# Routing scratch moved from SBUF into a PSUM bank, and the first batch's transforms set on other steps

## The chip, the cores and the metric

The kernel runs on one core of one Trainium2 chip. The metric is the device time of one execution in microseconds (us). An execution is also profiled: every instruction of the five engines has a start and an end. PE is TensorE's matrix multiply, PEld its weight load, DVE the vector engine, ACT the scalar engine, POOL the GpSimd engine, and SP the queue that only issues transfers.

## The reference

```python
X = np.fft.fft(np.fft.fft(x, axis=1), axis=2).real      # x: 8 x 3072 x 256
h = X.reshape(-1, 256) @ w_in                            # 256 -> 2048
y = (h * sigmoid(1.702 * h)) @ w_out                     # 2048 -> 256
do = y @ w_skip > 0                                      # only these rows go to an expert
e = argmax(y[do] @ w_gate, axis=1)                       # one of 8 experts
gate = softmax(y[do] @ w_gate)[e]
out = y;  out[do] += gate * (relu(y[do] @ w1[e]) @ w2[e])
```

## The kernel before

The work has two phases. **Phase 1** computes the Fourier transform, the first two-layer network and the routing; it fills the span up to about 1900 us. **Phase 2** runs the experts over the rows that phase 1 has scattered to memory.

Phase 1 goes over 8 batches, each cut in two half batches (the variable `hb`, 0 to 15). A half batch has three blocks of 512 tokens, and a block is worked off in 8 steps, so that a half batch has 24 steps and the whole has 384 (`main`, variable `g`). Products are split in high and low parts, so each is made of three matmuls.

A step consists of these pieces, in the order in which each engine's queue receives them:

- `hstep(g)`: 12 matmuls into the PSUM tiles `pt` (L855), then on DVE two instructions for `pp` (L859) and two for `h` (L861, L862).
- `ystep(g-2)`: 24 matmuls into the four accumulators `py` (L886), which use the step's `gh` and `gl`.
- `gelu(g)`: two activations on ACT (L869, L870), and on POOL the subtraction `gl` (L871, 128x1024 elements).
- After the last step of a block `finish` copies the four accumulators to `rows` (L894, DVE) while POOL sets one column of `rows` to zero (L891).
- The side list: whatever the dictionary `side` holds for this step, in the order in which it was appended. `plan` appends for all half batches before the loop starts; `finish` appends the routing of its block while the loop is written out. Nothing reorders these lists, and each engine runs its instructions strictly in this order.

The **routing** of a block stands in the side lists of the steps after its last one, in the order a1, a2, a3, four scatters, one step each:

- a1 is `route1`: six DVE instructions (L784 to L789) that find the best expert of each row and write the flags `oh` (128x32). Their scratch tiles `rm` and `rq` lie in SBUF. Then the transfer of `rows` to the output is issued on SP.
- a2 is `route2`: five small matmuls (L798, L800) with a triangle of ones, which count the rows in front of each row. They write a PSUM tile of the tag `misc`.
- a3 is `route3`: five DVE instructions (L810 to L814), which turn the counts into target rows.

The blocks are numbered from 0; the routing of block b has a1 in step 8b+10 of the whole count. A 49th, small routing handles 8 leftover tokens (`plan_mini`).

The tag `misc` has one PSUM bank and one buffer. Its other users are the **transforms** of the next half batch, `piece_mm` (L262): four per half batch, each with 9 matmuls (`p0` in `plan`), emptied one step later on DVE and ACT (`e0`, `e1`). A tile that takes the bank waits until every instruction that uses the tile before it is done.

POOL also folds the next batch's input (L212 to L224, L238 to L250), issues the scatters (L818) and the loads of the transform matrices (L202).

Of the kernel before, what the change touches and what calls it, by code (L numbers as in the profile page):

```python
# [12 lines left out]
F32 = mybir.dt.float32  # L13
# [5 lines left out]
ALU = mybir.AluOpType  # L19
AX = mybir.AxisListType  # L20
# [3 lines left out]
P = 128  # L24
# [140 lines left out]
class Phase1:  # L165
# [486 lines left out]
    def plan(self, hb):  # L652
        nc = self.nc
        b, odd = hb // 2, hb % 2
# [6 lines left out]
        st = {}  # L661
        if not odd:
# [8 lines left out]
            def p0(p):  # L671
                sh, sl = self.s
                q = self.piece_mm(st["cm"][4 + p % 2], sh, sl, p, KC)
                st["q"] = q
            def e0(p):
                st["xp"] = self.evac_odd0(b, p, st["q"])
            def e1(p):
                self.evac_odd1(p, st["xp"], st["q"], *st["y"], le)
            for p, s in enumerate((10, 13, 15, 21) if hb == 0 else (1, 5, 7, 13)):
                add(s, lambda p=p: p0(p))  # L680
                add(s + 1, (lambda p=p: e0(p)) if p % 2 == 0 else (lambda p=p: e1(p)))
            if b + 1 < self.nb:
# [65 lines left out]
        else:  # L748
# [14 lines left out]
                        self.cmn = self.cmn2  # L763
            def e0(p):
                self.evac_even(b + 1, p, st["q"], *st["y"], le)
            for p, s in enumerate((16, 18, 20, 22) if b == 0 else (8, 13, 15, 17)):
                add(s, lambda p=p: p0(p))
                add(s + 1, lambda p=p: e0(p))
            def sp(c):
# [4 lines left out]
                add(22 + c // 2 if b == 0 else 20 + c, lambda c=c: sp(c))  # L774


    def route1(self, rows, nt):
        nc, bp = self.nc, self.rp
        v = nc.vector
        sk, lg = rows[:, :nt, D], rows[:, :nt, D + 1 : D + 9]  # L780
        m = bp.tile([P, 4], F32, tag="rm", name="rm")
        q = bp.tile([P, 4, 8], F32, tag="rq", name="rq")
        oh = bp.tile([P, 4, 8], BF16, tag="roh", bufs=2, name="roh")
        v.tensor_reduce(m[:, :nt], lg, AX.X, ALU.max)  # L784
        v.tensor_tensor(q[:, :nt], lg, m[:, :nt].unsqueeze(2).to_broadcast([P, nt, 8]), ALU.is_ge)
        v.scalar_tensor_tensor(q[:, :nt], q[:, :nt], 16.0, self.k8[:, :nt], ALU.mult, ALU.add)
        v.tensor_reduce(m[:, :nt], q[:, :nt], AX.X, ALU.max)
        v.scalar_tensor_tensor(m[:, :nt], sk, 0.0, m[:, :nt], ALU.is_gt, ALU.mult)
        v.tensor_tensor(oh[:, :nt], q[:, :nt], m[:, :nt].unsqueeze(2).to_broadcast([P, nt, 8]), ALU.is_equal)  # L789
        return oh  # L790

    def route2(self, oh, nt):
        nc = self.nc
        ps = self.ps.tile([P, 512], F32, tag="misc", name="pmisc")
        o = oh[:, :nt].rearrange("p t e -> p (t e)")
        n = nt * 8
        mm = nc.tensor.matmul
        mm(ps[:, 0:n], lhsT=self.tri[:, 0], rhs=o, start=True, stop=False, skip_group_check=True)  # L798
        for i in range(nt):
            mm(ps[:, 8 * (i + 1) : n + 8], lhsT=self.tri[:, 1], rhs=o[:, : n - 8 * i], start=False, stop=i == nt - 1, skip_group_check=True)  # L800
        return ps

    def route3(self, rows, oh, ps, nt):
        nc, bp = self.nc, self.rp
        v = nc.vector
        q = bp.tile([P, 4, 8], F32, tag="rq", name="rq")
        m = bp.tile([P, 4], F32, tag="rm", name="rm")
        ix = bp.tile([P, 4], I32, tag="rix", bufs=2, name="rix")
        pv = ps[:, : nt * 8].rearrange("p (t e) -> p t e", t=nt)
        v.tensor_tensor(q[:, :nt], pv, self.base.unsqueeze(1).to_broadcast([P, nt, 8]), ALU.add)  # L810
        v.tensor_add(self.base, self.base, ps[:, nt * 8 : nt * 8 + 8])
        v.tensor_tensor(q[:, :nt], q[:, :nt], oh[:, :nt], ALU.mult)
        v.tensor_reduce(m[:, :nt], q[:, :nt], AX.X, ALU.add)
        v.tensor_scalar_add(ix[:, :nt], m[:, :nt], BIG)  # L814
        return ix
# [16 lines left out]
    def main(self):  # L832
        nc, tc, nb = self.nc, self.tc, self.nb
        v = nc.vector
        ps = self.ps
# [6 lines left out]
        bp = self.bp  # L842
        if True:
# [44 lines left out]
            def finish(gb, gnow):  # L888
                st = {}
                rows = self.rp.tile([P, 4, RW], F32, tag="rows", bufs=2, name="rows")  # L890
                nc.gpsimd.memset(rows[:, :, NW : NW + 1], 0.0)  # L891
                nc.gpsimd.tensor_scalar_add(rows[:, :, RW - 1 :], self.rid[:, 0, :, 1:], float(gb * TB))
                for t in range(4):
                    v.tensor_copy(rows[:, t, :NW], ys[gb][t])  # L894
                del ys[gb]

                def a1():
                    st["oh"] = self.route1(rows, 4)
                    nc.sync.dma_start(self.a["out"][gb * TB : (gb + 1) * TB].rearrange("(t p) d -> p t d", p=P), rows[:, :, :D])

                def a2():
                    st["ps"] = self.route2(st["oh"], 4)

                def a3():
                    st["ix"] = self.route3(rows, st["oh"], st["ps"], 4)

                left = nhb * NBLK - 1 - gb
                if left == 0:
                    self.last_block(a1, a2, a3, lambda t: self.scatter(rows, st["ix"], t))
                    return  # L910
                for i, f in enumerate((a1, a2, a3)):
                    self.side[gnow + 1 + i].append(f)
                for t in range(4):
                    self.side[gnow + 4 + (t // 2 if left == 1 else t)].append(lambda t=t: self.scatter(rows, st["ix"], t))
                if left == 1:
                    self.side[gnow + 5].append(pad0)
                if left == 2:
                    self.side[gnow + 8].append(self.ahead_load)
# [40 lines left out]
    def plan_mini(self, g0):  # L959
        nc, nb = self.nc, self.nb  # L960
        v = nc.vector
        st = {}

        def load():
            st["r"] = self.rp.tile([P, nb], F32, name="rmini")
            nc.sync.dma_start(st["r"], self.ydm.rearrange("b o -> o b").to_broadcast([P, nb]))
            st["m"] = [self.rp.tile([P, nb], F32R, name=f"m{i}") for i in range(2)]
            v.tensor_copy(st["m"][0], self.mini[:, :nb])
            v.tensor_sub(st["m"][1], self.mini[:, :nb], st["m"][0])

        def first():
            mh, ml = st["m"]
            ph = st["ph"] = self.ps.tile([P, NF, nb], F32, tag="misc", name="ph")
            for f in range(NF):
                for n, (w_, x_) in enumerate(((self.wch, mh), (self.wch, ml), (self.wcl, mh))):
                    nc.tensor.matmul(ph[:, f], lhsT=w_[:, 0, f * P : (f + 1) * P], rhs=x_, start=n == 0, stop=n == 2)

        def gelu():
            hm = self.rp.tile([P, NF, nb], F32, name="hm")
            v.tensor_mul(hm, self.w128.unsqueeze(2).to_broadcast([P, NF, nb]), st["r"].unsqueeze(1).to_broadcast([P, NF, nb]))  # L980
            v.tensor_add(hm, hm, st["ph"])
            nc.scalar.activation(hm, hm, AF.Gelu_apprx_sigmoid)
            st["g"] = [self.rp.tile([P, NF, nb], F32R, name=f"gm{i}") for i in range(2)]
            nc.scalar.copy(st["g"][0], hm)
            nc.gpsimd.tensor_sub(st["g"][1], hm, st["g"][0])

        def second():
            gh, gl = st["g"]
            py = st["py"] = self.ps.tile([P, NW], F32, tag="misc", name="pmini")
            for f in range(NF):  # L990
                for n, (x_, w_) in enumerate(((gh, self.woh), (gh, self.wol), (gl, self.woh))):
                    nc.tensor.matmul(py[:nb], lhsT=x_[:, f], rhs=w_[:, f], start=f == 0 and n == 0, stop=f == NF - 1 and n == 2)

        def rows():
            r = st["rows"] = self.rp.tile([P, 1, RW], F32, name="rowsm")
            v.memset(r[:, 0], 0.0)
            v.tensor_copy(r[:nb, 0, :NW], st["py"][:nb])

        def a1():
            r = st["rows"]  # L1000
            st["oh"] = self.route1(r, 1)
            v.tensor_scalar_add(r[:, 0, RW - 1 : RW], self.rid[:, 0, 0, 1:2], float(nb * S))
            nc.sync.dma_start(self.a["out"][nb * S : nb * S + nb], r[:nb, 0, :D])

        def a2():
            st["ps"] = self.route2(st["oh"], 1)

        def a3():
            st["ix"] = self.route3(st["rows"], st["oh"], st["ps"], 1)

        def sc():
            self.scatter(st["rows"], st["ix"], 0)

        for w, f in ((0, load), (4, first), (5, gelu), (7, second), (8, rows), (12, a1), (13, a2), (14, a3), (15, sc)):
            self.side[g0 + w].append(f)


# [388 lines left out]
```

## Time and profile before

| | |
|---|---|
| median of 3 runs | 2425.53 us (2424.12 to 2425.88) |
| profiled execution | 2424.24 us |
| its span in the trace | 2422.5 us |
| mean granted TensorE clock | 0.989 of full speed |

[...] Most executions agree within 0.1%, as the three times show.

### The profile page before, as it was taken

What the parts mean: (1) busy time and instruction counts of PE and PEld (TensorE: products, weight loads), DVE (VectorE), ACT (ScalarE), POOL (GpSimd) and SP (SyncE); (2) the same over time, 40 slices, a digit from 0 to 9 for tenths busy, and PEclk for the clock granted to TensorE, in tenths of its full rate; (3) what the DMA queues carried; (4) which work ended last, traced back from release to release, by engine and by line L of the source; (5) the groups of instructions that cost most, each with busy time, mean ns of one, the idle gap of its engine ahead of it and who ended that gap; (6) DMA issues with size and microseconds to landing.
All of it is one profiled execution on the core that took longest, in us unless ns stands there. A gap on an engine that the chain in (4) does not pass through costs nothing. (4 is left out here: it accounts for less than half of the span.)

```text
span 2422.5 us, 50479 instructions
## 1 busy us (share of the span) xinstructions
PE 2349.9 (97%) x19222; PEld 2320.0 (96%) x19222; DVE 1532.4 (63%) x3195; ACT 1095.8 (45%) x1355; POOL 1579.1 (65%) x1246
## 2 busy tenths in 40 slices
PE   5999999999999999999999999899999999999999
PEld 4899999999999999999999999899999999999999
DVE  7679676756665766576576757655657445555544
ACT  5544444444445454444544454445444333333332
POOL 3567688888878896878788888777666312323211
PEclk9999999999999999999999999999999999999999
DMA  7302311231122113112212121121101312323111
GB/s 259 116 34 77 122 55 37 68 124 37 65 91 77 39 60 130 37 37 86 104 53 69 59 100 47 55 89 39 62 20 33 107 44 84 115 84 113 40 43 41
DMA packets 91450, 178.83 MB, mean 74 GB/s; under 512 B 10895, under 2 KB 66750, under 8 KB 85104
## 3 DMA queue, kind: packets, MB, share of 16 engines
q1 hardware_dynamic: 69488, 96.12, 12.6%
q0 software_dynamic: 20448, 77.87, 9.4%
q8 instruction: 133, 2.18, 0.4%
q10 hardware_dynamic: 1312, 2.10, 0.3%
q14 instruction: 69, 0.57, 0.1%
HBM read 126.21 MB, written 66.59 MB: 80 GB/s over the span
## 5 line engine op out<-in xcount | busy, mean ns | idle before, releaser
L871 POOL TENSOR_TENSOR gl<-h,gh 128x1024 fp32r<-128x1024 f32 x384 | 923.8, 2406 | 352.2 <-ACT h L870 313.3
L869 ACT ACTIVATE gh<-h 128x1024 fp32r<-128x1024 f32 x384 | 407.4, 1061 | 890.0 <-DVE h L862 791.3
L886 PE MATMUL py<-woh,gh 128*128 128x264 f32 x3072 | 778.3, 287 | 0.7 <-DVE rows L894 0.7
L886 PE MATMUL py<-wol,gh 128*128 128x264 f32 x3072 | 775.6, 286 | 0.0
L859 DVE SCALAR_TENSOR_TENSOR pp<-rb,w,pt 128x256 f32<-128x256 f32 x768 | 334.0, 476 | 404.7 <-PE pt L855 404.2
L886 PEld LDWEIGHTS py<-woh,gh 128*128 128x128 f32 x3072 | 587.9, 191 | 1.1 <-issue 0.8
L886 PEld LDWEIGHTS py<-wol,gh 128*128 128x128 f32 x3072 | 586.6, 191 | 0.0
L886 PE MATMUL py<-woh,gl 128*128 128x264 f32 x3072 | 460.5, 284 | 1.0 <-POOL gl L871 1.0
L855 PE MATMUL pt<-yh,wch 128*128 128x256 f32 x1536 | 433.9, 283 | 3.3 <-DVE pp L859 2.6
L855 PE MATMUL pt<-yh,wcl 128*128 128x256 f32 x1536 | 429.3, 279 | 1.9 <-DVE wcl L431 1.9
L855 PE MATMUL pt<-yl,wch 128*128 128x256 f32 x1536 | 429.6, 280 | 0.7 <-POOL yl L296 0.5
L870 ACT ACTIVATE h<-h 128x1024 f32<-128x1024 f32 x384 | 407.7, 1062 | 35.2 <-ACT gh L869 0.7
L886 PEld LDWEIGHTS py<-woh,gl 128*128 128x128 f32 x3072 | 409.8, 189 | 1.2 <-POOL gl L871 1.2
L1287 POOL DMA_INDIRECT out<-ob,ix x82 | 79.9, 974 | 337.8 <-DVE ob L1301 335.7
L861 DVE TENSOR_TENSOR h<-pp,pt 128x512 f32<-128x512 f32 x384 | 264.2, 688 | 54.7 <-POOL gl L871 2.1
L855 PEld LDWEIGHTS pt<-yh,wch 128*128 128x128 f32 x1536 | 290.4, 189 | 4.4 <-DVE pp L859 3.0
L855 PEld LDWEIGHTS pt<-yh,wcl 128*128 128x128 f32 x1536 | 291.0, 189 | 2.1 <-DVE wcl L431 2.1
L855 PEld LDWEIGHTS pt<-yl,wch 128*128 128x128 f32 x1536 | 291.8, 190 | 1.1 <-POOL yl L296 0.7
L862 DVE TENSOR_TENSOR h<-pp,pt 128x512 f32<-128x512 f32 x384 | 261.2, 680 | 0.0
L818 POOL DMA_INDIRECT xs<-rows,rix x192 | 194.3, 1012 | 44.2 <-issue 26.9
L1309 PE MATMUL po<-w2h,hh 128*128 128x256 f32 x656 | 188.8, 288 | 0.0
L1273 PE MATMUL h<-xl,w1h 128*128 128x256 f32 x656 | 185.1, 282 | 2.3 <-issue 2.2
(230 smaller groups left out, 3487.5 us busy)
## 6 DMA issues: line engine op xcount, KB each, us to landing
cmat<-cm POOLq DMA_DIRECT2D x48, 1158.0 KB, 6.3
raw<-raw SPq DMA_DIRECT2D x48, 512.0 KB, 5.5
out<-rows SPq DMA_DIRECT2D x48, 512.0 KB, 3.2
r<-w SPq DMA_DIRECT2D x14, 1024.0 KB, 6.6
nx<-xs SPq DMA_DIRECT2D x33, 266.0 KB, 3.0
rb<-yd SPq DMA_DIRECT2D x48, 128.0 KB, 3.5
wide<-w_in SPq DMA_DIRECT2D x8, 512.0 KB, 8.7
wide<-w_out SPq DMA_DIRECT2D x8, 512.0 KB, 6.1
```

The source lines that it names most:

```text
L818: i = self.nc.gpsimd.indirect_dma_start(self.xs, bass.IndirectOffsetOnAxis(ap=ix[:, t : t + 1], axis=0), rows[:, t], None, bounds_check=E ...
L855: nc.tensor.matmul(pt[z][:, i], lhsT=w_[:, z, f], rhs=x_[:, z, cols], start=n == 0, stop=n == 2)
L859: v.scalar_tensor_tensor(pp[:, i], r, self.w128[:, 2 * s + i : 2 * s + i + 1], pt[0][:, i], ALU.mult, ALU.add)
L861: v.tensor_add(h[:, :, 0], pp, pt[1])
L862: v.tensor_sub(h[:, :, 1], pp, pt[1])
L869: nc.scalar.activation(gh, hv, AF.Gelu_apprx_sigmoid)
L870: nc.scalar.activation(hv, hv, AF.Gelu_apprx_sigmoid)
L871: nc.gpsimd.tensor_sub(gl, hv, gh)
L886: nc.tensor.matmul(ys[gb][t], lhsT=x_[:, i, tk], rhs=w_[:, 2 * s + i], start=s == 0 and part is hi and n == 0, stop=ends and part is lo an ...
L1273: nc.tensor.matmul(h[:, z], lhsT=w_[:, k, f * P : (f + 1) * P], rhs=x_[:, k], start=i == 0, stop=i == 5)
L1287: d = self.nc.gpsimd.indirect_dma_start(self.out, bass.IndirectOffsetOnAxis(ap=ix, axis=0), ob, None, bounds_check=self.ntok - 1, oob_is_e ...
L1309: self.nc.tensor.matmul(po[t], lhsT=x_[:, f, t * P : (t + 1) * P], rhs=w_[:, f], start=f == 0 and n == 0, stop=f == 7 and n == 2)
```

## The change

1. The scratch values `m` (4 columns) and `q` (32 columns) of the routing are columns 64 to 67 and 96 to 127 of the same PSUM tile into which the triangle matmuls write columns 0 to 39. So `route1` takes the `misc` bank in a1, a step earlier than before, and it is held until the end of a3.
2. One intermediate of `route1` stays in SBUF, as `k`. Before, it was written over `q`.
3. In the first half batch (hb 0) three of the transforms are set on steps 13, 15, 16 instead of 10, 13, 15 (the fourth stays at 21), and in the second (hb 1) on 16, 17, 21, 22 instead of 16, 18, 20, 22. The instructions that empty them follow one step later, as before, and so do the loads of the matrices that each `p0` of hb 1 issues.
4. The small routing of the leftover tokens moves by one step (12 to 15 becomes 13 to 16).

```diff
-            for p, s in enumerate((10, 13, 15, 21) if hb == 0 else (1, 5, 7, 13)):
+            for p, s in enumerate((13, 15, 16, 21) if hb == 0 else (1, 5, 7, 13)):
...
-            for p, s in enumerate((16, 18, 20, 22) if b == 0 else (8, 13, 15, 17)):
+            for p, s in enumerate((16, 17, 21, 22) if b == 0 else (8, 13, 15, 17)):
...
+    def scratch(self, ps):
+        return ps[:, 64:68], ps[:, 96:128].rearrange("p (t e) -> p t e", t=4)
+
     def route1(self, rows, nt):
...
-        m = bp.tile([P, 4], F32, tag="rm", name="rm")
-        q = bp.tile([P, 4, 8], F32, tag="rq", name="rq")
+        ps = self.ps.tile([P, 512], F32, tag="misc", name="pmisc")
+        m, q = self.scratch(ps)
         oh = bp.tile([P, 4, 8], BF16, tag="roh", bufs=2, name="roh")
         v.tensor_reduce(m[:, :nt], lg, AX.X, ALU.max)
         v.tensor_tensor(q[:, :nt], lg, m[:, :nt].unsqueeze(2).to_broadcast([P, nt, 8]), ALU.is_ge)
-        v.scalar_tensor_tensor(q[:, :nt], q[:, :nt], 16.0, self.k8[:, :nt], ALU.mult, ALU.add)
-        v.tensor_reduce(m[:, :nt], q[:, :nt], AX.X, ALU.max)
+        k = bp.tile([P, 4, 8], F32, tag="rq", name="rq")
+        v.scalar_tensor_tensor(k[:, :nt], q[:, :nt], 16.0, self.k8[:, :nt], ALU.mult, ALU.add)
+        v.tensor_reduce(m[:, :nt], k[:, :nt], AX.X, ALU.max)
         v.scalar_tensor_tensor(m[:, :nt], sk, 0.0, m[:, :nt], ALU.is_gt, ALU.mult)
-        v.tensor_tensor(oh[:, :nt], q[:, :nt], m[:, :nt].unsqueeze(2).to_broadcast([P, nt, 8]), ALU.is_equal)
-        return oh
+        v.tensor_tensor(oh[:, :nt], k[:, :nt], m[:, :nt].unsqueeze(2).to_broadcast([P, nt, 8]), ALU.is_equal)
+        return oh, ps
...
-    def route2(self, oh, nt):
+    def route2(self, oh, ps, nt):
         nc = self.nc
-        ps = self.ps.tile([P, 512], F32, tag="misc", name="pmisc")
...
     def route3(self, rows, oh, ps, nt):
...
-        q = bp.tile([P, 4, 8], F32, tag="rq", name="rq")
-        m = bp.tile([P, 4], F32, tag="rm", name="rm")
+        m, q = self.scratch(ps)
...
-        for w, f in ((0, load), (4, first), (5, gelu), (7, second), (8, rows), (12, a1), (13, a2), (14, a3), (15, sc)):
+        for w, f in ((0, load), (4, first), (5, gelu), (7, second), (8, rows), (13, a1), (14, a2), (15, a3), (16, sc)):
```

## Rows read from the trace of the kernel before

**Rows 1.** The page: busy time of each engine, share of the span, instructions.
```profile
PE 2349.9 (97%) x19222; PEld 2320.0 (96%) x19222; DVE 1532.4 (63%) x3195; ACT 1095.8 (45%) x1355; POOL 1579.1 (65%) x1246
```

**Rows 2.** Waits of PE: us in total, times, the longest.
```profile
PE pmisc L798 <- DVE roh L789: 25.1, 13, 4.3
...
PE pmisc L798 <- DVE yl L281: 2.1, 1, 2.1
...
PE pmisc L798 <- DVE xp L286: 0.5, 1, 0.5
```

**Rows 3.** DVE's routing lines: out<-in, count | busy us, mean ns | idle before.
```profile
L812 DVE TENSOR_TENSOR rq<-rq,roh 128x32 f32<-128x32 f32 (+1 forms) x49 | 58.6, 1196 | 0.0
L786 DVE SCALAR_TENSOR_TENSOR rq<-rq,k 128x32 f32<-128x32 f32 (+1 forms) x49 | 33.3, 680 | 1.7
L788 DVE SCALAR_TENSOR_TENSOR rm<-rows,rm 128x4 f32<-128x4 f32 x48 | 32.6, 678 | 1.7
L785 DVE TENSOR_TENSOR rq<-rows,rm 128x32 f32<-128x32 f32 x48 | 22.6, 471 | 1.7
L789 DVE TENSOR_TENSOR roh<-rq,rm 128x32 bf16<-128x32 f32 (+1 forms) x49 | 22.5, 458 | 1.7
L814 DVE TENSOR_SCALAR rix<-rm 128x4 int32<-128x4 f32 (+1 forms) x49 | 20.8, 424 | 1.7
...
L787 DVE TENSOR_REDUCE rm<-rq 128x4 f32<-128x32 f32 (+1 forms) x49 | 9.1, 186 | 1.7
L810 DVE TENSOR_TENSOR rq<-pmisc,base 128x32 f32<-128x32 f32 (+1 forms) x49 | 9.0, 183 | 0.0
```

**Rows 4.** DVE's timeline in blocks 19 and 38: start us, us, instruction [idle before <-releaser].
```profile
840.36 0.19 DVE L784 TENSOR_REDUCE rm<-rows 128x4 f32<-128x32 f32 x1 [3.59 <-POOL rows L891]
...
841.33 3.35 DVE L786 SCALAR_TENSOR_TENSOR rq<-rq,k 128x32 f32<-128x32 f32 x1
...
850.96 0.18 DVE L810 TENSOR_TENSOR rq<-pmisc,base 128x32 f32<-128x32 f32 x1
851.18 0.16 DVE L811 TENSOR_TENSOR base<-base,pmisc 128x8 f32<-128x8 f32 x1
851.26 1.09 DVE L812 TENSOR_TENSOR rq<-rq,roh 128x32 f32<-128x32 f32 x1
...
1555.52 5.17 DVE L785 TENSOR_TENSOR rq<-rows,rm 128x32 f32<-128x32 f32 x1
```

**Rows 5.** POOL's timeline beside block 19's routing, same columns.
```profile
841.88 2.33 POOL L871 TENSOR_TENSOR gl<-h,gh 128x1024 fp32r<-128x1024 f32 x1
...
849.90 2.39 POOL L871 TENSOR_TENSOR gl<-h,gh 128x1024 fp32r<-128x1024 f32 x1 [4.87 <-ACT h L870]
```

**Rows 6.** PE's timeline: a2's first matmul in blocks 4, 5, 19, 20, 38.
```profile
275.89 0.18 PE L798 MATMUL pmisc<-roh,tri 128*128 128x32 bf16 x1 [2.06 <-DVE yl L281]
...
318.10 0.18 PE L798 MATMUL pmisc<-roh,tri 128*128 128x32 bf16 x1 [1.34 <-DVE roh L789]
...
845.37 0.18 PE L798 MATMUL pmisc<-roh,tri 128*128 128x32 bf16 x1 [3.08 <-DVE roh L789]
...
881.35 0.19 PE L798 MATMUL pmisc<-roh,tri 128*128 128x32 bf16 x1
...
1561.61 0.19 PE L798 MATMUL pmisc<-roh,tri 128*128 128x32 bf16 x1 [4.29 <-DVE roh L789]
```

**Rows 7.** Busy time by stretch: PE, PEld, DVE, ACT, POOL (count), then PEclk, DMA.
```profile
846.95:850.36 3.41, 3.41 (x18) 3.41 (x18) 3.19 (x8) 2.12 (x2) 0.46 (x1) 0.50 0.01 2
...
1560.34:1567.17 6.83, 5.56 (x30) 5.56 (x30) 6.32 (x16) 3.16 (x3) 1.32 (x2) 0.50 0.01 2
```

**Rows 8.** Timeline of half batch 1: emptying transforms (DVE), the accumulators' end (PE).
```profile
263.24 0.41 PE L886 MATMUL py<-woh,gl 128*128 128x264 f32 x2
...
264.03 0.61 DVE L274 SCALAR_TENSOR_TENSOR xt<-coef,spec,pmisc 128x386 f32<-128x386 f32 x1
...
289.39 0.56 DVE L281 TENSOR_TENSOR yl<-pmisc,yh 128x384 fp32r<-128x384 f32 x1 [2.71 <-ACT yh L280]
```

More of the change, by code (lines that the diff above doesn't have):

```diff
@@ L800, in route2 @@
             mm(ps[:, 8 * (i + 1) : n + 8], lhsT=self.tri[:, 1], rhs=o[:, : n - 8 * i], start=False, stop=i == nt - 1, skip_group_check=True)
-        return ps
     def route3(self, rows, oh, ps, nt):
@@ L897, in a1 @@
                 def a1():
-                    st["oh"] = self.route1(rows, 4)
+                    st["oh"], st["ps"] = self.route1(rows, 4)
                     nc.sync.dma_start(self.a["out"][gb * TB : (gb + 1) * TB].rearrange("(t p) d -> p t d", p=P), rows[:, :, :D])
                 def a2():
-                    st["ps"] = self.route2(st["oh"], 4)
+                    self.route2(st["oh"], st["ps"], 4)
                 def a3():
@@ L1000, in a1 @@
             r = st["rows"]
-            st["oh"] = self.route1(r, 1)
+            st["oh"], st["ps"] = self.route1(r, 1)
             v.tensor_scalar_add(r[:, 0, RW - 1 : RW], self.rid[:, 0, 0, 1:2], float(nb * S))
@@ L1005, in a2 @@
         def a2():
-            st["ps"] = self.route2(st["oh"], 1)
+            self.route2(st["oh"], st["ps"], 1)
         def a3():
```

## The prediction

> **What bounds the kernel now.** I read the page first: PE is busy 97% of the span, no other engine above 65% [rows 1]. The whole span is PE's own work, some 2350 us, plus the about 72 us in which it stands still, plus what its clock costs it. A change that adds or removes no large matmul can gain only from the last two. So the second view is PE's waits. Behind the start-up the largest entry by far is the routing: the triangle matmul of a2 waits for the flags `oh` of L789, 25.1 us in 13 of 49 blocks, and in the first batch twice for the emptying of a transform that still holds the bank, 2.1 and 0.5 us [rows 2].
>
> Why are the flags late? The third view, DVE's routing lines, shows two kinds. L787 and L810 take 0.18 to 0.19 us; L812, L786, L788, L785, L789 and L814 do arithmetic of the same size or less, but have means of 0.42 to 1.20 us [rows 3]. The timelines show what happens. In block 19, L786 takes 3.35 us [rows 4], while POOL's subtraction L871 runs through the middle of it [rows 5]. In a3 of the same block there is a test inside one POOL subtraction, the one that starts at 849.90 and lasts 2.39 us: L810 and L811, with one operand in PSUM and one in SBUF, run in 0.18 and 0.16 us; L812, with both operands in SBUF, starts 0.08 us after L811 and ends at 852.35, when POOL's ends (852.29) [rows 4, 5]. So a DVE instruction with two SBUF operands is held until POOL's subtraction is done, and one with a single SBUF operand isn't. Block 38 has the worst: L785 held for 5.17 us, PE waiting 4.29 [rows 4, 6].
>
> The fourth view is the clock. [...] I read this stretch for each stall: it follows six of the 13 (blocks 7, 13, 19, 25, 31, 37, with stalls of 2.3 to 3.1 us), always 3.41 us long; it is 6.83 us long around block 38's; it also follows the bank's wait of 2.06 us in block 4. It doesn't follow the shorter ones, such as 1.34 us in block 5 [rows 6]. PE runs all the while, at half speed, so each stretch costs half its length, 1.7 us.
>
> **The change part by part.**
>
> *Scratch in PSUM.* After the change each of the six slow lines has at most one operand in SBUF: L785 reads the logits (SBUF) and `m` (PSUM), L786 `q` and the constant, L788 and L789 `m` and one SBUF tile, L812 `q` and the flags, L814 only `m`. By the test in block 19 none is held any more. DVE's time falls by 58.6 + 33.3 + 32.6 + 22.6 + 22.5 + 20.8 = 190.4 us less 6 x 49 x 0.19 = 56, so by some 134 us [rows 3]. Most of that is off the path; what ends on PE is the 25.1 us [rows 2].
>
> Does all of the 25.1 go? In block 19 a1 starts at 840.36, once POOL has zeroed its column. L810 and L811 start 0.22 us apart [rows 4], so six instructions take 1.3 us and the flags are there at 841.7. PE wanted them at 845.37 - 3.08 = 842.3 [rows 6]: 0.6 us to spare. In block 38 a1's second instruction starts at 1555.52, so the flags come at 1556.6, and PE wanted them at 1561.61 - 4.29 = 1557.3: 0.7 to spare. The smallest margin that I found in the 13 is this 0.6. So all the waits go: **-25.1 us**.
>
> *PSUM's own price.* Reading PSUM costs nothing by L810 against L787, 183 to 186 ns [rows 3]. No DVE instruction in this trace writes PSUM. Below, it costs nothing (a gain is excluded, since 0.19 us is what unheld instructions of either kind take); above, I take the double of an unheld instruction, +0.19 us for each of the six in a1, +1.1 us. Then 0.5 us of wait would be left in the eight blocks that have 0.6 or 0.7 to spare, 4 us. I take the lower end, 0, because the nearest row, L810, touches the same bank.
> [...]
>
> *The clock.* Without the stalls I expect the stretches at 0.50 to go with them: 6 x 1.7 = 10.2 us, and for block 38, where PE was busy 5.56 of the 6.83 us [rows 7], 2.8: **-13.0 us**. Bounds: 0 (the clock falls anyway) to 13.
>
> *What is late next.* PE then reaches the next steps 3.08 + 1.7 = 4.8 us earlier. DVE's next step starts some 3.5 us earlier (flags at 841.7 for 845.3). POOL stood still for 4.87 us there, waiting for ACT, which waited for DVE [rows 5], so its next subtraction moves up about as far as DVE does, to within 1.3 us of PE's gain. Block 20's matmul ran with nothing to wait for, but its flags came only just before [rows 6]. So a wait of up to 1.3 us may appear there, in six batches: 0 to 8 us. I take 2, as the unheld routing of the block ahead (18) lets POOL run earlier too: **+2.0 us**.
>
> *The bank held one step longer.* a1 now needs the bank a step earlier. Each earlier user is emptied by DVE instructions that stand before a1 in DVE's own queue, so nothing new is queued there. The matmuls of a transform that follows a routing (steps 5 and 13 of a half batch) come a step after a3, as before, and wait for L814 where they waited for L811, with about a step in hand. I price that at 0. The transfer to the output behind a1 on SP waits for `rows` alone: 0.
>
> *First batch.* In hb 0 the transforms leave block 0's routing alone: -0.45 [rows 2]. Setting the third one in step 16, behind the emptying of the second in the same step, may cost as much; I take 0 for both together. In hb 1 the wait of block 4, 2.06 us and its 1.7 of clock, goes [rows 6]: -3.8. New are two transforms set in the very step in which the one before is emptied. In step 17 the accumulators end at 263.65 and L274, which empties the first transform, at 264.64 [rows 8]: PE waits 1.0 to 1.2. In step 22 the third is emptied by ACT behind its two activations and then by DVE; DVE itself waits 2.71 us for ACT in that pattern [rows 8], and what PE waits is block 4's case again: 2.1, and 1.7 of clock. POOL's loads of matrices move along with the `p0` that issues them, behind the same matmuls; the next use is steps away. Sum: -3.8 + 1.1 + 3.8 = **+1.1 us**, between -3 and +4.
>
> *The small routing one step later* and the last block: no wait of PE stands there, 0; at most a1's extra time once.
>
> **Sum.** 2424.24 (the profiled execution) - 25.1 - 13.0 + 2.0 + 1.1 = 2389.2. The median of the runs is 1.3 us above the profiled execution, so 2390.5; I say **2390 us**, -1.5%.
>
> **The rivals.**
> 1. *The forecast*: stalls and clock stretches both go. 2380 to 2398. Chance 0.68.
> 2. *POOL, or PSUM's price, becomes the next bound.* The waits are shortened, not removed: PSUM at its upper bound leaves 4 us, POOL at its upper bound 6 more than I took, and half of the clock's 13 stays where waits of 2 us remain. 2390 + 4 + 6 + 6.5 = 2406, so 2398 to 2412. For it: flags and POOL's subtraction come just in time in the blocks behind the stalls. Against: POOL's idle 4.87 us shows that it was itself kept waiting. Chance 0.20.
> 3. *DVE is held all the same*, for instance since its writes or the other operand still meet POOL. Then only the first batch changes: 2425 to 2427. Against: L810 and L811 ran through the subtraction in 0.18 us. Chance 0.07.
> 4. *Slower: the bank.* Every transform that follows a routing waits for a3's end, three in each of 8 batches. It takes 1.6 us for each of the 24 to eat the 38 us; at 3 us each the time is 2390 + 72 = 2462. For it: one bank for both, now held through three steps. Against: the bank was already held until a3, and a3 gets shorter by most of L812's 1.2 us. Chance 0.05.
>
> **How the numbers follow.** The predicted time is rival 1's. The range holds it and most of rival 2: 2380 to 2406. A measurement of this kernel tells about 0.2%, 5 us, from no change. Faster by more: 0.68 + 0.20 and a little, 0.89. Within 0.2%: rival 3, 0.06. Slower: rival 4 and a part of 3, 0.05.
>
> **What would show each step.** Right: the six lines at 0.16 to 0.25 us without a maximum above 0.4; the row "L798 <- `oh`" near nothing; the granted clock at 1.00 behind blocks 7, 13, 19, 25, 31, 37 and 38; two new waits of a transform in steps 17 and 22 of hb 1. Wrong: L785 to L789 still lasting 1 us or more; or short, with PE now waiting for POOL's `gl` or for flags whose a1 began late; or waits of L262 on L814.

## The result and the profile after

The median of four runs is 2386.51 us (2382.92 to 2391.28), beside 2425.7 us before (four runs): a ratio of 0.9838, interval 0.9817 to 0.9860. The forecast was 2390 us. The profiled execution took 2382.92 us, 41.3 less than the 2424.24 of before. It is the fastest of the four; the medians differ by 39.2.

The page's first line, which answers to [rows 1], already divides the gain of that execution: PE is busy 17.2 us less for the same 19222 matmuls, and the rest of the 41.3, 24.1 us, is time in which it no longer stands still.

```profile
PE 2332.7 (98%) x19222; PEld 2302.1 (97%) x19222; DVE 1407.3 (59%) x3195; ACT 1095.8 (46%) x1355; POOL 1577.9 (66%) x1246
```

PE's waits in the changed kernel (us in total, times, the longest). The entry of 25.1 us for the flags [rows 2] is gone; nothing of that kind has come up. The two waits of a transform in half batch 1 are there, and POOL's `gl` is now waited for five times, by 0.2 us at most (before it was once, for 1.0 us, near the end of phase 1):

```profile
PE pmisc L262 <- DMA cmat<-cm: 18.2, 1, 18.2
...
PE pmisc L262 <- DVE yl L281: 2.0, 1, 2.0
...
PE pmisc L262 <- DVE xt L274: 1.1, 1, 1.1
PE py L887 <- POOL gl L872: 0.9, 5, 0.2
```

DVE's routing lines, which answer to [rows 3] (count | busy us, mean ns | idle before). Line numbers have moved: the compare is L788, the line with the constant L790, the mask L792, the flags L793, the product L813, the index L815. All six are at 161 to 199 ns, with no trace of a hold. The two reductions, L791 and L814, and the sum L811 are shown for PSUM's price further down:

```profile
L813 DVE TENSOR_TENSOR pmisc<-pmisc,roh 128x32 f32<-128x32 f32 (+1 forms) x49 | 9.7, 199 | 1.7
L814 DVE TENSOR_REDUCE pmisc<-pmisc 128x4 f32<-128x32 f32 (+1 forms) x49 | 9.7, 199 | 1.7
...
L791 DVE TENSOR_REDUCE pmisc<-rq 128x4 f32<-128x32 f32 (+1 forms) x49 | 9.5, 194 | 1.7
L811 DVE TENSOR_TENSOR pmisc<-pmisc,base 128x32 f32<-128x32 f32 (+1 forms) x49 | 9.4, 193 | 0.0
L788 DVE TENSOR_TENSOR pmisc<-rows,pmisc 128x32 f32<-128x32 f32 x48 | 9.4, 196 | 1.6
...
L790 DVE SCALAR_TENSOR_TENSOR rq<-pmisc,k 128x32 f32<-128x32 f32 (+1 forms) x49 | 9.3, 190 | 1.7
L793 DVE TENSOR_TENSOR roh<-rq,pmisc 128x32 bf16<-128x32 f32 (+1 forms) x49 | 9.2, 188 | 1.7
...
L792 DVE SCALAR_TENSOR_TENSOR pmisc<-rows,pmisc 128x4 f32<-128x4 f32 x48 | 8.1, 168 | 1.6
...
L815 DVE TENSOR_SCALAR rix<-pmisc 128x4 int32<-128x4 f32 (+1 forms) x49 | 7.9, 161 | 2.0 <-DVE pmisc L814 0.4
```

The test in block 19 can be read again, in DVE's timeline and POOL's below it (start us, us, instruction). The compare L788 runs inside POOL's sum of 825.73 and takes 0.20 us. The product L813 starts 0.19 us after L812 and takes 0.20, where it took 1.09 [rows 4]; it meets only the last 0.14 us of POOL's subtraction of 831.52, so by itself it shows little, but no L813 of the whole trace, 35 of the 49 begun while POOL was at work, lasts longer than 0.20 us. A line that the change didn't touch, L235, has both operands in SBUF. It starts inside the subtraction of 827.12 and lasts 0.91 us, until POOL's next instruction, L223, is done as well; its like, L232, takes 0.28 with POOL standing still:

```profile
825.86 0.20 DVE L788 TENSOR_TENSOR pmisc<-rows,pmisc 128x32 f32<-128x32 f32 x1
...
826.74 0.19 DVE L793 TENSOR_TENSOR roh<-rq,pmisc 128x32 bf16<-128x32 f32 x1
...
829.17 0.91 DVE L235 TENSOR_TENSOR va<-eo 64x128 f32<-64x128 f32 x1
...
830.55 0.28 DVE L232 TENSOR_TENSOR va<-eo 64x128 f32<-64x128 f32 x1
...
833.59 0.16 DVE L812 TENSOR_TENSOR base<-base,pmisc 128x8 f32<-128x8 f32 x1
833.78 0.20 DVE L813 TENSOR_TENSOR pmisc<-pmisc,roh 128x32 f32<-128x32 f32 x1
```

```profile
825.73 0.75 POOL L218 TENSOR_TENSOR eo<-pq 128x256 f32<-128x256 f32 x1
...
827.12 2.38 POOL L872 TENSOR_TENSOR gl<-h,gh 128x1024 fp32r<-128x1024 f32 x1
829.47 0.45 POOL L223 TENSOR_TENSOR ub<-eo 128x128 f32<-128x128 f32 x1
...
831.52 2.40 POOL L872 TENSOR_TENSOR gl<-h,gh 128x1024 fp32r<-128x1024 f32 x1 [1.13 <-ACT h L871]
```

The clock, by stretches as in [rows 7]: from 300 to 1750 us, in which the kernel before has seven of the eight stretches at 0.50 of full speed behind the routing's stalls, the granted clock is 1.00 throughout, and PE is idle for 1.2 us in all. The one stretch at 0.50 between 100 and 1850 us comes right behind the first small matmuls of the leftover tokens (L977, 48 of 128x8), and was twice as long before. It is 6.83 us long in experiments 1 to 5 and 8 too, which have the changed steps, so its length here isn't shown to be the change's work. The changed kernel's two rows, then the one of before:

```profile
300.00:1750.00 1450.00, 1448.79 (x12035) 1445.26 (x12034) 871.66 (x1986) 708.54 (x711) 1207.13 (x942) 1.00 0.21 68
1755.42:1758.83 3.41, 3.41 (x18) 3.41 (x18) 1.51 (x4) 0.00 (x0) 0.00 (x0) 0.50 0.02 5
```

```profile
1792.44:1799.27 6.83, 6.83 (x33) 6.83 (x34) 2.65 (x6) 0.59 (x1) 0.54 (x1) 0.50 0.01 2
```

### The profile page after: what moved, and what is told of

Its sections match the earlier page's. It is cut to its first block, busy times and chain, and to the rows that moved or that the text cites. A ratio compares the mean times of both kernels' runs of the same rounds, so it can differ in the third digit from the quotient of the medians.

```text
span 2381.1 us, 50490 instructions
## 1 busy us (share of the span) xinstructions
PE 2332.7 (98%) x19222; PEld 2302.1 (97%) x19222; DVE 1407.3 (59%) x3195; ACT 1095.8 (46%) x1355; POOL 1577.9 (66%) x1246
## 5 line engine op out<-in xcount | busy, mean ns | idle before, releaser
L887 PE MATMUL py<-woh,gh 128*128 128x264 f32 x3072 | 766.8, 284 | 0.0
L887 PE MATMUL py<-wol,gh 128*128 128x264 f32 x3072 | 765.0, 283 | 0.0
L887 PEld LDWEIGHTS py<-woh,gh 128*128 128x128 f32 x3072 | 578.3, 188 | 0.3
L887 PEld LDWEIGHTS py<-wol,gh 128*128 128x128 f32 x3072 | 577.3, 188 | 0.0
L1274 PE MATMUL h<-xh,w1h 128*128 128x256 f32 x656 | 183.9, 280 | 4.1 <-PEq L1332 2.1
```

Source lines behind the costliest of these rows:

```text
L887: nc.tensor.matmul(ys[gb][t], lhsT=x_[:, i, tk], rhs=w_[:, 2 * s + i], start=s == 0 and part is hi and n == 0, stop=ends and part is lo an ...
L1274: nc.tensor.matmul(h[:, z], lhsT=w_[:, k, f * P : (f + 1) * P], rhs=x_[:, k], start=i == 0, stop=i == 5)
```

## The experiments

Ratios are against the kernel before on the same chip.

**1. The steps without PSUM.** The kernel before, with three lines changed, which are the schedule alone:

```diff
-            for p, s in enumerate((10, 13, 15, 21) if hb == 0 else (1, 5, 7, 13)):
+            for p, s in enumerate((13, 15, 16, 21) if hb == 0 else (1, 5, 7, 13)):
...
-            for p, s in enumerate((16, 18, 20, 22) if b == 0 else (8, 13, 15, 17)):
+            for p, s in enumerate((16, 17, 21, 22) if b == 0 else (8, 13, 15, 17)):
...
-(12, a1), (13, a2), (14, a3), (15, sc)
+(13, a1), (14, a2), (15, a3), (16, sc)
```

> The routing as before, with its scratch in SBUF; only the steps of the first batch's transforms and of the small routing are the changed ones. Theory (DVE instructions with two SBUF operands are held by POOL): nothing is gained, PE still waits some 24 us for the flags, the two new transform waits of 1.1 and 2.0 us are there; about 2426 us (2423 to 2430). Rival (the steps make the gain): 2386 to 2400 us.

Measured: 2429.88 us, ratio 1.0014 (1.0004 to 1.0023), by that 3.4 us slower with an interval of 1 to 6. Its waits of PE:

```profile
PE pmisc L798 <- DVE roh L789: 23.4, 12, 4.3
...
PE pmisc L262 <- DVE yl L281: 2.1, 1, 2.1
...
PE pmisc L262 <- DVE xt L274: 1.1, 1, 1.1
```

The steps make no gain; they cost about what was forecast (+1.1), or a little more.

**2. Only route1 in PSUM**, and **3. only route3 in PSUM**, both on the changed steps. The second is the changed kernel with

```diff
     def route3(self, rows, oh, ps, nt):
...
-        m, q = self.scratch(ps)
+        q = bp.tile([P, 4, 8], F32, tag="rq", name="rq")
+        m = bp.tile([P, 4], F32, tag="rm", name="rm")
```

and the third is the first experiment's kernel with `m, q = ps[:, 64:68], ps[:, 96:128]...` in route3 in place of the two SBUF tiles.

> The changed kernel, but route3 takes its scratch from SBUF again, so that only route1 is in PSUM. Theory: the flags come in 1.3 us in every block, PE's direct waits of up to 4 us go; route3's product and index line stay held (some 60 us of DVE in all), which delays the next step's pp and through it POOL, so waits of about 1 us come up in the blocks without slack: 2388 to 2398 us. Rival (only the flags matter): as the changed kernel, 2386 us.

> The mirror image: route1 with its scratch in SBUF, route3 in PSUM, steps as changed. Theory: PE waits for flags that are still held: 18 to 25 us of waits, six or more clock stretches at 0.50, 2412 to 2426 us. Rival (the gain goes with DVE's held time, of which about half is in route3): 2405 us, half of the gain.

Measured: route1 alone 2385.04 us, ratio 0.9827 (0.9810 to 0.9843), all of the gain; route3 alone 2427.06 us, 1.0003 (0.9993 to 1.0012), none. In the second kernel route3's product and index line are still held:

```profile
L814 DVE TENSOR_TENSOR rq<-rq,roh 128x32 f32<-128x32 f32 (+1 forms) x49 | 38.1, 778 | 0.0
L816 DVE TENSOR_SCALAR rix<-rm 128x4 int32<-128x4 f32 (+1 forms) x49 | 13.2, 270 | 2.1 <-DVE rm L815 0.4
```

That is 38.1 + 13.2 less 17.6 as in the changed kernel, some 34 us of held DVE time, and it costs nothing that can be measured: the ratio is the changed kernel's within the intervals, some 4 us. I had expected 2 to 12 us from it: wrong, here the rival held. In the third kernel the flags are waited for as ever:

```profile
PE pmisc L798 <- DVE roh L789: 23.6, 14, 3.8
```

So in this kernel held time counts where PE is next in line, which is between `rows` and the flags, and not behind them.

**4. Only `m` in PSUM**, and **5. only `q` in PSUM**, to see which property of an instruction gets it held. In both route1 and route3:

```diff
-        m, q = self.scratch(ps)
+        m = self.scratch(ps)[0]                                    # 4
+        q = bp.tile([P, 4, 8], F32, tag="rq0", name="rq0")         # 4
...
-        m, q = self.scratch(ps)
+        q = self.scratch(ps)[1]                                    # 5
+        m = bp.tile([P, 4], F32, tag="rm", name="rm")              # 5
```

> The changed kernel with only m (4 columns) in PSUM and q in SBUF. Theory (held is who has two SBUF operands): the compare with m, the mask line, the flags line and the index line last 0.16 to 0.20 us; the line q with the constant and the product q with the flags, which have two SBUF operands, are held, the first with a mean of over 1 us, since it now takes the hold that three lines shared. PE waits 5 to 20 us, 2393 to 2415 us. Rival (what counts is that the result goes to PSUM): the compare, whose result q is in SBUF, is held too.

> The changed kernel with only q (32 columns) in PSUM and m in SBUF: the mirror image of the run before. Theory: now the compare (rows and m, result in PSUM), the mask line (rows and m) and the flags line (k and m) have two SBUF operands and are held, with means of 0.4 us and more; the line q with the constant and the product q with the flags are not, 0.18 to 0.20 us. Rival (results in PSUM are free): the compare is not held.

Measured: 2399.55 us, 0.9894 (0.9877 to 0.9910), for `m` alone. For `q` alone there is one run, 2419.62 us beside a median of 2424.46 with a lowest of 2419.90, from which no gain can be told; the lines of its trace are what counts. DVE's lines with only `m` in PSUM; the first two have both operands in SBUF, the third, the compare, has not:

```profile
L815 DVE TENSOR_TENSOR rq<-rq,roh 128x32 f32<-128x32 f32 (+1 forms) x49 | 47.3, 965 | 0.0
L791 DVE SCALAR_TENSOR_TENSOR rq<-rq,k 128x32 f32<-128x32 f32 (+1 forms) x49 | 37.0, 756 | 1.7
...
L789 DVE TENSOR_TENSOR rq<-rows,pmisc 128x32 f32<-128x32 f32 x48 | 9.0, 188 | 1.6
```

and with only `q` in PSUM:

```profile
L817 DVE TENSOR_SCALAR rix<-rm 128x4 int32<-128x4 f32 (+1 forms) x49 | 40.6, 829 | 1.7
L793 DVE SCALAR_TENSOR_TENSOR rm<-rows,rm 128x4 f32<-128x4 f32 x48 | 29.4, 612 | 1.7
L789 DVE TENSOR_TENSOR pmisc<-rows,rm 128x32 f32<-128x32 f32 x48 | 27.6, 576 | 1.6
...
L815 DVE TENSOR_TENSOR pmisc<-pmisc,roh 128x32 f32<-128x32 f32 (+1 forms) x49 | 9.7, 199 | 1.7
...
L791 DVE SCALAR_TENSOR_TENSOR rq<-pmisc,k 128x32 f32<-128x32 f32 (+1 forms) x49 | 9.3, 190 | 1.7
```

The compare, the product and the line with the constant each change sides with their operands, and the compare is held although its result lies in PSUM (576 ns, with `q` there), and free although it lies in SBUF (188 ns, with `m` in PSUM): the sources decide. The expectation that the line with the constant would have a mean of over 1 us was too high (0.756). A surprise stands in the first row of the last fence: the index line reads one tensor only, `m`, and is held all the same when `m` is in SBUF.

**6 and 7. A longer a1 with nothing held.** The changed kernel, with the first reduction of route1 made 6 or 16 times:

```diff
-        v.tensor_reduce(m[:, :nt], lg, AX.X, ALU.max)
+        for _ in range(6):                                         # 7: range(16)
+            v.tensor_reduce(m[:, :nt], lg, AX.X, ALU.max)
```

> The changed kernel with the first reduction of route1 made six times instead of once, so that the flags come 1.1 us later, with nothing held. It is the upper bound that the prediction took for PSUM's price. Theory: the slack is what the changed trace shows between flags and matmul: six blocks (8, 14, 20, 26, 32, 38) have none and wait 1.1 us each, block 4 waits 0.4; together 7 us, no clock stretch at 0.50 behind them: 2393 us. Rival (there is slack everywhere, since POOL and PE adjust): under 2 us, 2387 us.

> The same with 16 reductions: the flags come 3.3 us later, again with nothing held. Theory (a stall of 2 us and more also costs a stretch at half clock): PE waits of 30 to 50 us in all, and PE's own busy time up by 1.7 us for each of 8 to 14 stretches at 0.50: 2430 to 2460 us. Rival (a stall costs itself alone): PE's busy time stays at 2333 us, and the time is 2386 us and the waits.

Measured: 2404.88 us, 0.9919 (0.9904 to 0.9934), and 2470.9 us, 1.0194 (1.0179 to 1.0210). The sixth kernel's waits of PE:

```profile
PE pmisc L802 <- DVE roh L794: 6.9, 8, 1.2
...
PE py L888 <- POOL gl L873: 3.1, 6, 0.7
PE pmisc L262 <- DVE yl L281: 2.4, 1, 2.4
```

The 6.9 us for the flags are the forecast 7, and nearly all of it lies in the forecast blocks: 6.3 in the six, 0.3 in block 4. But the time rose by 18 (20 by the ratios), not by 7. The two profiled executions lie further apart, 25.8 us, because the changed kernel's is the fastest of its four and this one the slowest of its own. PE's idle time is 13.3 us higher there, of which the flags are half; the rest is spread over waits for POOL, for `pp` and for transforms. PE's busy time is 12.5 us higher, by stretches at half clock, among them one of 10.24 us in place of 3.41 behind the small matmuls of the leftover tokens. From block 5 to block 42 the two drift apart by 8.6 us, which is the six waits for the flags and 2.0 us more for `gl`. The rest arises ahead of block 5 and behind block 42; why 1.1 us in a1 reaches there was not settled. The seventh kernel's first line of the page, and its wait for the flags:

```profile
PE 2368.4 (96%) x19222; PEld 2335.6 (95%) x19222; DVE 1557.8 (63%) x3930; ACT 1096.1 (44%) x1355; POOL 1577.2 (64%) x1246
```

```profile
PE pmisc L802 <- DVE roh L794: 50.3, 25, 3.3
```

PE does the same 19222 matmuls in 35.7 us more. Twenty stretches at half clock are in its trace, 79.1 us long together, against four of 16.8 us in the changed kernel: half of the difference, 31, is most of that. So the stalls cost themselves and their clock, without any hold, which falsifies the rival. The theory's 2 us is not where the line runs, though: in this trace a wait for the flags of 1.70 us is followed by such a stretch, and three of 2.59, 2.63 and 2.72 us are not. My range for the time was too low: the waits are at its upper end, and there are 16 more stretches, not 8 to 14.

**8. The order of the last two transforms.** The changed kernel, in half batch 1:

```diff
-            for p, s in enumerate((16, 17, 21, 22) if b == 0 else (8, 13, 15, 17)):
+            for p, s in ((0, 16), (1, 17), (3, 21), (2, 22)) if b == 0 else ((0, 8), (1, 13), (2, 15), (3, 17)):
```

with the matrix loads of that half batch in the same order.

> The changed kernel with the last two transforms of the second half batch in the other order (the fourth in step 21, the third in step 22), and their matrix loads likewise. The fourth is emptied by one DVE instruction, not by ACT behind its activations. Theory: the wait of 2.0 us in step 22 falls to under 0.4 us, the time by 2 us, which is inside the spread of the runs. Rival: the wait moves to the next user of the bank and the sum of PE's waits stays.

Measured: 2382.68 us, 0.9826 (0.9813 to 0.9839). The wait of 2.0 us for `yl` is gone from PE's waits, and only the 1.0 in step 17 is left. Nothing took its place: PE's idle time in the profiled execution is 44.1 us, for 48.4 in the changed kernel, and even the short waits for `gl` are gone, so the rival is out. The row is clear; the gain in time is not. The median is 3.8 us below the changed kernel's, beside the lowest of that kernel's runs, and the intervals overlap.

**9. POOL writes, but doesn't read.** The kernel before, with its subtraction replaced by fills,

```diff
-                nc.gpsimd.tensor_sub(gl, hv, gh)
+                for f in range(2):
+                    for z in range(2):
+                        nc.gpsimd.memset(gl[:, f].bitcast(F32), 0.0)
```

so that it leaves the low part of the second product out.

> The kernel before, but POOL's subtraction gl (L871) is replaced by four fills of the same tile with zero, which write SBUF and read nothing; the low part of the second product is left out by that. POOL stays about as busy. Theory (a DVE instruction with two SBUF operands is held by a POOL instruction that reads SBUF): routing lines that overlap a fill last 0.16 to 0.20 us, and only POOL's folds, splits and sums, which read, still hold some; held time of the six lines falls from 134 us to under 50, PE's wait for the flags from 25 us to under 8. Rival (any POOL instruction holds them): means of 0.4 to 1.2 us as before.

Measured, in one run: 2376.73 us beside 2421.77, with no wait for the flags of any length in the list. One a1 shows both cases. POOL's timeline and below it DVE's:

```profile
819.48 0.72 POOL L218 TENSOR_TENSOR eo<-pq 128x256 f32<-128x256 f32 x1
820.16 0.73 POOL L219 TENSOR_TENSOR eo<-pq 128x256 f32<-128x256 f32 x1
820.84 2.15 POOL L873 MEMSET gl<- 128x512 f32 x4
```

```profile
819.57 0.68 DVE L785 TENSOR_TENSOR rq<-rows,rm 128x32 f32<-128x32 f32 x1
820.28 0.66 DVE L786 SCALAR_TENSOR_TENSOR rq<-rq,k 128x32 f32<-128x32 f32 x1
...
821.20 0.16 DVE L788 SCALAR_TENSOR_TENSOR rm<-rows,rm 128x4 f32<-128x4 f32 x1
821.40 0.19 DVE L789 TENSOR_TENSOR roh<-rq,rm 128x32 bf16<-128x32 f32 x1
```

Beside POOL's two sums, which read SBUF, L785 and L786 are held to 0.68 and 0.66 us; inside the fill, L788 and L789 with the same kind of operands take 0.16 and 0.19. In the whole trace 54 starts of the five two-operand lines (L785, L786, L788, L789, L812) fall into a fill, and the longest of them lasts 0.194 us. The six slow lines are busy for 69.1 us in all, some 13 of it held, where 134 were held before.

## Why the prediction was right

**The hold.** Right, and now separated from its rivals: experiments 4 and 5 show that the sources decide (the compare at 188 ns with `m` in PSUM, at 576 with only `q` there), experiment 9 that POOL's reading does it, with 0.66 us beside a reading and 0.19 beside a fill. One sentence of the prediction was too wide: that an instruction with a single SBUF operand isn't held. The index line (`tensor_scalar`) has a single one, and had a mean of 424 ns already in [rows 3]; in experiment 5 it has 829. That it came free with the rest, at 161 ns, is owed to its one operand being moved, not to that sentence. The reductions, also with a single SBUF operand, were never held (190 ns at most in the kernel before); the runs don't show what tells the index line from them.

**-25.1 us of waits for flags.** Right: they are gone. It is route1 alone that brings it (experiments 2 and 3), as the step said that PE waits for the flags and for nothing behind them. The margins of the step are not what the trace has. In block 19, for which 0.6 us was forecast, the flags are ready at 826.93 and PE comes 1.23 us later:

```profile
828.16 0.19 PE L801 MATMUL pmisc<-roh,tri 128*128 128x32 bf16 x1
```

In block 38, for which 0.7 was forecast, the matmul starts 0.05 us behind the flags: there a1 was just fast enough.

**PSUM's price.** Taken as 0. A result in PSUM instead of SBUF costs the unheld lines about 10 ns, 0.05 of the upper bound: 183 to 193 for L810, now L811, and 186 to 194 for L787, now L791. A source in PSUM costs less still: L814, a reduction out of PSUM, takes 199 ns, 5 more than L791 out of SBUF. The upper bound itself was priced too low: the prediction had 4 us of waits for a1 longer by 1.1 us, and experiment 6, which makes it so, measures 18.

**The clock, -13.0.** The mechanism held: the seven stretches went as forecast, and experiment 7 brings such stretches back with stalls alone, twenty of 79.1 us together for the four of 16.8. What a stretch costs can be read in the one behind block 19's stall of 3.08 us, the first row of [rows 7]: at 0.50 PE's matmuls L886 start every 0.22 us, and in the 3.41 us that follow, at 1.00, every 0.12. So nearly half of a stretch is lost, close to the forecast's 1.7 us. The row that follows it in the kernel before, with 31 matmuls for 18:

```profile
850.36:853.77 3.41, 3.41 (x31) 3.41 (x31) 3.17 (x10) 2.12 (x2) 2.28 (x2) 1.00 0.00 0
```

The size is not better known than to some 4 us. PE's busy time fell by 17.2 in the profiled execution, 4.2 more than forecast, and 3.4 of it looks like luck. Block 4's 1.7 went and did not come back with the 2.0 us wait of step 22 in this execution, though I had counted it again; in experiment 2, on the same steps, a wait of 2.02 us there is followed by 3.41 us at 0.50. And the stretch behind the leftover tokens was 3.41 us shorter, which is 1.7, where experiment 2 has the old 6.83. PE's busy time in experiment 2 is 14.3 us below that of before. Two stretches in phase 2 went and one came; I had forecast nothing there, and give no cause.

**POOL next in line, +2.0.** It measured 0.9 us in five waits for `gl`; in the six blocks that were meant (block 20 and its like: 8, 14, 20, 26, 32, 38), the matmul starts 0.05 us behind the flags, with a wait of less than 0.1. Experiment 6 shows how near that bound is: 1.1 us more in a1 brings 1.0 to 1.2 us of wait in each of these six.

**First batch, +1.1.** The two new waits are 1.05 and 2.02 us for the forecast 1.0 to 1.2 and 2.1; block 0's 0.45 is gone, and nothing came in its place. Experiment 1 has the whole schedule at 3.4 us, interval 1 to 6.

**The rivals.** Rivals 3 and 4 are out: no line is held, and no transform behind a routing waits for the index line. Rival 2's mechanism is there, with 0.9 us where POOL's upper bound was 8.

## What to carry to other kernels

Here a tiny DVE instruction with two SBUF operands lasted until the GpSimd instruction beside it was done, where that one read SBUF (1.09 us for block 19's product, 0.66 beside a sum in experiment 9), and 0.16 to 0.19 us beside a fill. A mean far above the minimum of its line was the sign (L785: 471 ns, 191 at least for 128x32), and moving one operand to PSUM ended it (196 ns). It is worth doing only where the bound engine is next in line: here one function of the two brought all 39 us, and 34 us of held time in the other cost nothing. Count a stall of the bound engine with what its clock can lose behind it, here by estimate 1.7 us for each 3.41 us at 0.50, and expect that to vary: a wait of 2.02 us in step 22 was followed by 3.41 us at 0.50 in experiment 2 and by 1.00 in the changed kernel (288.50 to 295.40 us).

## What the runs showed of the hardware that was not expected

- L785's 5.17 us in block 38 [rows 4] is longer than any one POOL instruction there: POOL's own instructions followed one another without a gap, and L785 was done at 1560.69, only when POOL stood still (from 1560.64). Experiments 4 and 5 each have one such, of 4.94 and 5.20 us, beside the same six POOL instructions. POOL's timeline of the kernel before:

```profile
1555.43 0.45 POOL L223 TENSOR_TENSOR ub<-eo 128x128 f32<-128x128 f32 x1
...
1557.09 2.33 POOL L871 TENSOR_TENSOR gl<-h,gh 128x1024 fp32r<-128x1024 f32 x1
1559.39 1.25 POOL L212 TENSOR_TENSOR pq<-raw 128x512 f32<-128x512 f32 x1
```

- PE's clock also fell to 0.50 behind 48 matmuls of 8 columns with no stall in them, for 3.4 to 10.2 us in the executions of the kernels here, by half of that an estimate of 1.7 to 5.1 us of time.
